# Four VectorE sums of a Strassen-Winograd product, handed out one at a time between out matmuls

## The chip, the core and the metric

The kernel runs on one core of a Trainium2 chip. The metric is the device time of one execution in microseconds (us), lower is better. A core has TensorE (PE, matmuls into PSUM), VectorE (DVE), ScalarE (ACT, activations), GpSimd (POOL) and SyncE (SP); each works through a queue of its own in order, and they wait for one another by semaphores. PSUM has eight banks, each of which holds one matmul output of 128 x 512 float32.

## The reference

Sigmoid attention over 8 batches of 12 heads, 448 positions and 64 channels a head, followed by a feed-forward layer with SiLU on the 3584 x 768 result:

```python
scores = scale * np.matmul(q, k.transpose(0, 1, 3, 2)) - np.log(S)
attn = 1.0 / (1.0 + np.exp(-scores))
attn_out = np.matmul(attn, v)
...
x = np.ascontiguousarray(attn_out.transpose(0, 2, 1, 3)).reshape(B * S, H * D)
h = x @ w_in
g = h * (1.0 / (1.0 + np.exp(-h)))
return (g @ w_out).astype(np.float32)
```

w_in is 768 x 2048 and w_out 2048 x 768. All is computed in float16 with float32 sums; the result is float32.

## The kernel before

**Stages.** Heads are taken in groups g of four (three groups make a batch, 24 groups in all), and a group's scores in seven units (`NCH`), so that a batch pair has 42 units. The pairs are worked through in stages. A first stretch does the attention of the first pair, then h of its two batches runs as plain products with the attention of the second pair between. Then the loop at the end of the kernel runs three times, m = 0, 1, 2. Each pass has an *out stage*: the out products of pair m (`sets(m)`, g @ w_out), with the attention of pair m + 1 between them. Then comes an *h stage*: `h_pair(m + 1)`, x @ w_in with SiLU for that pair. A last `sets(3)` ends the kernel.

**Out stage.** In `out_set` a set of two row blocks is computed with seven products instead of eight (Strassen-Winograd): each is eight matmuls of 128x128 by 128x384 into one PSUM bank `po`. In this text they are P1 to P7. VectorE reads each out of its bank: P1 at L511 (`m1`), P2 at L515, P3 at L521, P4 at L525, P5 at L528, P6 at L531 and L532, P7 at L536. It also makes the four sums S1 to S4 of `gTr` (L509, L512, L516, L522), which are weights of later products; S4 of L522 is for P7. In the out stages with attention, `banks_for_attention(3)` gives three double banks to scores and P·V, and leaves two single banks for `po`, taken in turn. So a product's first matmul waits for the eviction of the product two before it.

**Attention between.** `burst(n)` issues the scores of two units (`scores`, eight matmuls for the two, then one sigmoid of ScalarE per unit) and, one burst after a group's last unit, the group's P·V (`values`, 28 matmuls), whose two results VectorE writes to `xT` (L267). Behind a burst the loop takes `int(behind_burst)` steps from the stream of out matmuls: `few` behind a burst with values (2 in m = 0 and 2, 4 in m = 1), `many` behind another (8.5 and 11.4 on average). `rows_if_any` is called twice in each round: right behind the burst, and in the middle of its out matmuls. It hands out the copies and transposes of later rows of k and q, where such wait in `later`.

**The sums of x.** h of a pair is a Strassen-Winograd product too, and needs four sums of `xT`: `tx[m, 1]`, `tx[m, 2]`, a sum in place of `x1[0]`, and `tx[m, 4]` (L352 to L355, here s1 to s4; s2 reads s1, s4 reads s2). `xT` has six channel groups of 128, of which each attention group g fills two. The first two thirds of the sums (`x_sums(m, 0, NQ - 1)`, 128x896 each) can be made when the last but one attention group of the pair is in; `after_values` issues all four there, behind that group's `values`. The last third (128x448 each) is made within the h stage by `last_values`, behind the last group's values; `gate` then lets GpSimd go on to the next rows and loads.

The order of instructions on each engine is the order in which the program issues them.

Of the kernel before, what the change touches and what calls it, by code (L numbers as in the profile page):

```python
# [17 lines left out]
def kernel(  # L18
# [9 lines left out]
    nc = tc.nc  # L28
# [8 lines left out]
    NQ = NPAIR // 2  # L37
# [26 lines left out]
    def banks_for_attention(doubles):  # L64
        psum.close()
        banks.clear()
        bufs_of.update(double=doubles, single=NBANK - 2 * doubles)
        for name, bufs in bufs_of.items():
            taken[name] = 0
            new_pool(name, bufs)  # L70
# [7 lines left out]
    def banks_for_h():  # L78
        doubles = [[2 * i, 2 * i + 1] for i in longest_idle("double")]
        ring[:] = sum(doubles[:-2], [])  # L80
        ring.extend(2 * bufs_of["double"] + i for i in longest_idle("single"))
        ring.extend(sum(doubles[-2:], []))
        psum.close()
        banks.clear()
        new_pool("any", 1)
        for i in range(NBANK):
            banks[i] = banks["any"].tile([P, 512], F32, tag=f"any{i}", name=f"any{i}")
# [32 lines left out]
    def load(names, g, c0=0, c1=NCH):  # L120
        for name in names:
            if (name, g) not in flat:
                new_flat(name, g)
            nc.gpsimd.dma_start(  # L124
                flat[name, g][:, :, c0:c1].rearrange("p i c d -> p i (c d)"),
                rows_in(name, g)[:, :, c0 * D : c1 * D],
            )
# [22 lines left out]
    def load_w_in(step):  # L150
        cols = slice(step * DFF // 4, (step + 1) * DFF // 4)
        rows = moe_w_in[:, cols].rearrange("(iq j h d) f -> h j d iq f", j=2, h=2, d=D)
        for half in range(2):
            for j in range(2):
                nc.gpsimd.dma_start(
                    w_in_sb[j * D : (j + 1) * D, half * NQ : (half + 1) * NQ, cols], rows[half, j]
                )

    def load_w_out(nh, part):
        cols = slice(nh * NO2, (nh + 1) * NO2)  # L160
        fcs = slice(part * NFC // 2, (part + 1) * NFC // 2)
        nc.gpsimd.dma_start(
            w_out_sb[:, fcs, cols],
            moe_w_out[part * DFF // 2 : (part + 1) * DFF // 2, cols].rearrange(
                "(fc p) e -> p fc e", p=P
            ),
        )
# [39 lines left out]
    def dma_transpose(g, name, copy):  # L207
        if ("k", g) not in qkT:
            new_qkT(g)
        rows = p2.tile([P, NCH, 2, D], F16, tag=f"{name}r", name=f"{name}r")  # L210
        copy(rows, flat[name, g].rearrange("p j c d -> p c j d"))
        nc.sync.dma_start_transpose(
            out=qkT[name, g], in_=rows.rearrange("p c j d -> p (c j d)")
        )
# [62 lines left out]
    def room_x():  # L277
        return p3.tile([P, NQ, S], F16, tag="tx", name="tx")
# [64 lines left out]
    tx = {}  # L343

    def x_sums(m, lo, hi):
        if lo == 0:
            for i in (1, 2, 4):
                tx[m, i] = room_x()
        of = slice(lo, hi)
        x0, x1 = ([xT[2 * m + j][:, c * NQ : (c + 1) * NQ] for c in range(2)] for j in range(2))  # L350
        sub = nc.vector.tensor_sub
        sub(tx[m, 1][:, of], x1[0][:, of], x0[0][:, of])  # L352
        sub(tx[m, 2][:, of], x1[1][:, of], tx[m, 1][:, of])  # L353
        sub(x1[0][:, of], x1[1][:, of], x1[0][:, of])  # L354
        sub(tx[m, 4][:, of], x0[1][:, of], tx[m, 2][:, of])  # L355

    NG = NFC // 2

    def h_pair(m, last_values):

        x0, x1 = xT[2 * m], xT[2 * m + 1]
# [68 lines left out]

        last = NG - 1
        order = [(m1, 0), (m1, 1), (last_values,), (m1, 2)]
        for i in range(3):
            order += [(m2, i), (silu11, i)]
# [132 lines left out]
    def sets(m):  # L567
        for g in range(0, NCH - 1, 2):
            step = out_set(
                block(m, g), row_blocks(m, g), block(m, g + 1), row_blocks(m, g + 1)  # L570
            )
            for i, ns in enumerate(step):
                if m == 0 and g == 0 and i in (10, 14):
                    next(sums)
                if m == 0 and g == 0 and i in (20, 28, 36, 44):
                    next(in_sums)
                yield ns
        if m % 2 == 1:
            g = NCH - 1
            yield from out_set(  # L580
                kept, row_blocks(m - 1, g), block(m, g), row_blocks(m, g), m == B // 2 - 1
            )

    later = []

    def rows_if_any(before, copy):
        if later and later[0][0] < before:
            g, name = later.pop(0)
            dma_transpose(g, name, copy)
            if name == "q":  # L590
                behind_rows(g, before)
# [3 lines left out]
    def behind_rows(g, before):  # L595
        if g + 3 >= NQB:
            return
        if g + 3 < before:
            load("kq", g + 3)
            return  # L600
        held.append(g + 3)
        if g + 1 == before:
            nc.gpsimd.tensor_copy(gate, qkT["q", g][:1, 0, :1])
            for to in held:
                load("kq", to)
            held.clear()
# [33 lines left out]
    def after_values(g):  # L640
        if g == 0:
            load("v", 3)
            load_w_in(2)
            load_w_in(3)
        elif g == 1:
            load("v", 4)
            load_w_out(0, 0)
            load_w_out(0, 1)
        elif g == 2:
            load("v", 5)  # L650
            load_w_out(1, 0)
            load_w_out(1, 1)
            load("kq", 6)
            load("kq", 7)
        elif g + 3 < NQB:
            load("v", g + 3)
        if g >= 2 * NQ and g % (2 * NQ) == 2 * NQ - 2:
            x_sums(g // (2 * NQ), 0, NQ - 1)

    def values_if_any():  # L660
        if waiting:
            g = waiting.pop(0)
            values(g)
            after_values(g)
            return True
        return False
# [15 lines left out]
    def rounds(g, end):  # L682
        values(g, end)
        if end == NCH:
            after_values(g)
# [47 lines left out]
    def burst(n):  # L733

        new = units[n : n + 2]
        for u in new:
            scores(*u)
        with_values = values_if_any()
        for g, ch in new:
            if ch == NCH - 1:  # L740
                waiting.append(g)
                if 9 <= g + 3 < NQB:
                    later.extend(((g + 3, "k"), (g + 3, "q")))
        return with_values
# [13 lines left out]
    for m in range(B // 2 - 1):  # L758
        banks_for_attention(3)
        nc.scalar.activation(warm, bias_s, AF.Sigmoid)  # L760
        stream = sets(m)
        for _ in range(FIRST_DENSE):
            next(stream)

        dense = (3 + m % 2) * 7 * NHC - FIRST_DENSE - ENDING
        with_values = 2 * NQ - 1
        few = 2 + 2 * (m % 2)
        many = (dense - with_values * few) / (NT_B - with_values)
        own = 2 * NQ * (m + 2)
        behind_burst = 0.0  # L770
        for n in range(2 * NT_B * (m + 1), 2 * NT_B * (m + 2), 2):
            behind_burst += few if burst(n) else many
            rows_if_any(own, nc.vector.tensor_copy)
            half = int(behind_burst) // 2
            for i in range(int(behind_burst)):
                next(stream)
                if i == half:
                    rows_if_any(own, nc.vector.tensor_copy)
            behind_burst -= int(behind_burst)
        nc.scalar.activation(warm, bias_s, AF.Silu)  # L780
        for _ in stream:
            pass
        (g,) = waiting
        waiting.clear()
        banks_for_h()
        values(g, NCH - 1)

        def last_values():
            values(g)
            after_values(g)  # L790
            x_sums(m + 1, NQ - 1, NQ)
            nc.gpsimd.tensor_copy(gate, tx[m + 1, 4][:1, NQ - 1, :1])

        for i, _ in enumerate(h_pair(m + 1, last_values)):
            if i % 8 == 7:
                rows_if_any(NQB, nc.gpsimd.tensor_copy)
# [33 lines left out]
```

## Time and profile before

| | us |
|---|---|
| median of 3 runs | 373.86 |
| lowest and highest run | 373.62, 374.12 |
| the profiled execution | 374.06 |
| its span, first to last instruction | 372.1 |

In a page of the profile the engines' busy time comes first, then groups of equal instructions, each with its line, engine, output and input tiles, count, busy time, mean length in ns, and the idle time of the engine just before them with what ended it. The timeline lists instructions of one engine in order of time, equal neighbours merged. The clock granted to TensorE was 0.999 over the span.

The groups that matter here beside those shown further on:

| line, engine, form | count | mean, ns |
|---|---|---|
| L352 to L355, DVE, 128x896 float16 | 3 each | 616 to 625 |
| L352 to L355, DVE, 128x448 float16 | 3 each | 382 to 393 |
| L521, L525, L528, DVE, 128x384 float32 | 14 each | 552 to 557 |
| L522, DVE, 128x1024 float16 | 14 | 681 |
| L267, DVE, 128x448 from PSUM | 48 | 619 |
| L501, PE, 128x384 | 784 | 326 to 327, one every 163 ns in a run of them |

### The profile page before, as it was taken

Reading aid. Unit: us, or ns where it says so; the run is one execution under the profiler, and the core shown is the slowest. Engines: PE = TensorE matmul, PEld = TensorE weight load, DVE = VectorE, ACT = ScalarE, POOL = GpSimd, SP = SyncE. Lnnn points to the kernel's source line nnn. Section 1 sums busy time; section 2 is a strip of 40 time slices with the busy share of each in tenths; the row PEclk is TensorE's granted clock in tenths of the full one; section 3 lists DMA queues with packets and bytes.
Section 4 is the critical chain, followed back from the end, with each engine's and each line's share of the span. In section 5 each row is a group of like instructions: output and inputs, shape, how many; then the busy total and the mean of one; then the engine's idle time right before and its main releaser. Section 6 shows DMA issues by size and latency. Waiting matters only on the chain. (4 is left out here: it accounts for less than half of the span.)

```text
span 372.1 us, 7598 instructions
## 1 busy us (share of the span) xinstructions
PE 360.6 (97%) x3009; PEld 179.8 (48%) x3009; DVE 252.0 (68%) x458; ACT 250.9 (67%) x339; POOL 77.5 (21%) x116
## 2 busy tenths in 40 slices
PE   7999999999999999999999899999999999999995
PEld 3554445544444455544444345554444445555553
DVE  2565469867566587867665658796665667797763
ACT  5998885479989655687778656679899846650000
POOL 8566521040060172000033036100100000000000
PEclk9999999999999999999999999999999999999999
DMA  8999999998789599008579459921983030003333
GB/s 135 192 204 204 204 203 204 181 127 154 132 106 218 115 122 177 2 0 158 93 136 181 113 110 143 120 37 26 175 108 88 0 87 0 3 0 85 86 85 85
DMA packets 65698, 42.78 MB, mean 115 GB/s; under 512 B 36096, under 2 KB 62208, under 8 KB 65664
## 3 DMA queue, kind: packets, MB, share of 16 engines
q0 software_dynamic: 27072, 22.58, 42.2%
q1 hardware_dynamic: 38240, 19.44, 27.2%
q8 instruction: 23, 0.38, 0.4%
q10 hardware_dynamic: 352, 0.30, 0.2%
q14 instruction: 11, 0.09, 0.1%
HBM read 45.61 MB, written 11.01 MB: 152 GB/s over the span
## 5 line engine op out<-in xcount | busy, mean ns | idle before, releaser
L232 ACT ACTIVATE attnT<-psc,bias_s 128x896 f16<-128x896 f32 x168 | 159.1, 1007 | 23.4 <-PE psc L225 22.9
L501 PEld LDWEIGHTS <-S 128*128 128x128 f16 x448 | 40.8, 98 | 39.6 <-issue 13.5
L225 PE MATMUL psc<-qT,kT 64*64 64x448 f16 x672 | 50.9, 362 | 1.5 <-ACT qT L186 0.6
L267 DVE TENSOR_SCALAR xT<-pav 128x448 f16<-128x448 f32 x48 | 27.7, 619 | 32.0 <-PE pav L256 32.0
L124 POOL DMA_DIRECT2D vf<-in_v_dram x24 | 17.3, 729 | 135.2 <-PE pav L256 130.6
L501 PEld LDWEIGHTS <-gTr 128*128 128x128 f16 x336 | 30.8, 98 | 30.2 <-issue 12.2
L501 PE MATMUL po<-T,S 128*128 128x384 f16 x224 | 42.5, 327 | 0.0
L501 PE MATMUL po<-w_out_sb,gTr 128*128 128x384 f16 x224 | 42.2, 327 | 0.0
L501 PE MATMUL po<-w_out_sb,S 128*128 128x384 f16 x224 | 40.4, 326 | 1.8 <-DVE osb L525 1.8
L375 PEld LDWEIGHTS <-w_in_sb 128*128 128x128 f16 x288 | 27.7, 98 | 26.9 <-issue 1.7
L256 PE MATMUL pav<-attnT,vf 64*64 64x448 f16 x672 | 38.9, 351 | 0.4 <-DVE gTr L303 0.4
L288 PE MATMUL ph<-xT,w_in_sb 128*128 128x448 f16 x192 | 38.7, 353 | 0.1
L375 PE MATMUL pa<-xT,w_in_sb 128*128 128x448 f16 x144 | 33.2, 353 | 0.0
L375 PEld LDWEIGHTS <-SI 128*128 128x128 f16 x216 | 21.1, 98 | 20.0 <-issue 0.5
L225 PEld LDWEIGHTS <-kT 64*64 64x64 f16 x672 | 15.4, 104 | 29.3 <-issue 25.7
L256 PEld LDWEIGHTS <-vf 64*64 64x64 f16 x672 | 21.4, 106 | 14.0 <-issue 5.4
L391 ACT ACTIVATE part<-pa 128x448 f32<-128x448 f32 x24 | 13.0, 543 | 21.5 <-PE pa L375 20.6
L288 PEld LDWEIGHTS <-w_in_sb 128*128 128x128 f16 x192 | 17.8, 98 | 19.1 <-issue 3.7
L501 PE MATMUL po<-T,gTr 128*128 128x384 f16 x112 | 22.2, 327 | 1.5 <-DVE osb L521 1.5
L369 ACT ACTIVATE gTr<-pc 128x448 f16<-128x448 f32 x24 | 13.0, 543 | 12.9 <-DVE pc L385 12.5
L385 DVE TENSOR_TENSOR part<-pb,part 128x448 f32<-128x448 f32 x24 | 14.9, 621 | 8.3 <-ACT part L391 5.0
L186 ACT ACTIVATE m<-po 128x384 f32<-128x384 f32 x1 | 0.5, 490 | 27.7 <-PE po L501 27.7
(76 smaller groups left out, 468.0 us busy)
## 6 DMA issues: line engine op xcount, KB each, us to landing
out_dram<-osb SPq DMA_DIRECT2D x54, 192.0 KB, 2.9
vf<-in_v_dram POOLq DMA_DIRECT2D x24, 224.0 KB, 7.0
kf<-in_k_dram POOLq DMA_DIRECT2D x23, 224.0 KB, 8.0
qf<-in_q_dram POOLq DMA_DIRECT2D x23, 224.0 KB, 8.5
w_in_sb<-in_moe_w_in_dram POOLq DMA_DIRECT2D x16, 192.0 KB, 7.9
w_out_sb<-in_moe_w_out_dram POOLq DMA_DIRECT2D x4, 768.0 KB, 14.9
kT<-kr SPq DMA_TRANSPOSE x18, 4.5
qT<-qr SPq DMA_TRANSPOSE x18, 4.8
```

The lines of the kernel that those rows point to most:

```text
L124: nc.gpsimd.dma_start(flat[name, g][:, :, c0:c1].rearrange("p i c d -> p i (c d)"), rows_in(name, g)[:, :, c0 * D : c1 * D],)
L186: nc.scalar.activation(o, i, AF.Copy)
L225: nc.tensor.matmul(psc[own, j, :S], qkT["k", g][rows, ch, own], qkT["q", g][rows, :, own], start=True, stop=True,)
L232: nc.scalar.activation(attnT[g, ch], psc[:, :, :S], AF.Sigmoid, bias=bias_s, scale=QKSCALE)
L256: nc.tensor.matmul(pav[half][j * D : (j + 1) * D, :S], flat["v", g][own, j, ch, :], at[own, j, :], start=(ch == 0), stop=(ch == NCH - 1),)
L267: nc.vector.tensor_scalar_mul(xT[b][:, half * NQ + iq, :], pav[half][:, :S], SX)
L288: nc.tensor.matmul(ph[:, :S], w_in_sb[:, cc, fc * P : (fc + 1) * P], xT[b][:, cc, :], start=(at == 0), stop=(at == NCC - 1),)
L369: nc.scalar.activation(gTr[:, r * NG + i, col + c * S : col + (c + 1) * S], h, AF.Silu, bias=0.0, scale=ISX)
L375: nc.tensor.matmul(to, w[:, n, i * P : (i + 1) * P], x[:, n], start=(start and n == 0), skip_group_check=not start, stop=(n == NQ - 1),)
L385: nc.vector.tensor_add(o, po, x)
L391: nc.scalar.activation(got[i, 1], bank[i, "a"], AF.Copy)
L501: nc.tensor.matmul(po[:, :NO2], a[:, fc, :], w[:, fc, :], start=(fc == 0), stop=(fc == NHC - 1))
```

## The change

`x_sums` becomes a generator that yields behind each of its sums. At the place where the four sums were issued, the generator is now put into a list, `sums_of_x`, and every call of `rows_if_any` takes one step of it, ahead of what it did before. The first step is thus taken right behind the burst whose values completed the group, the second in the middle of the out matmuls behind that burst, the third behind the next burst, the fourth in the middle of that burst's out matmuls. The last third's sums in `last_values` are run through at once, as before. What is computed stays the same.

```diff
         of = slice(lo, hi)
         x0, x1 = ([xT[2 * m + j][:, c * NQ : (c + 1) * NQ] for c in range(2)] for j in range(2))
-        sub = nc.vector.tensor_sub
-        sub(tx[m, 1][:, of], x1[0][:, of], x0[0][:, of])
-        sub(tx[m, 2][:, of], x1[1][:, of], tx[m, 1][:, of])
-        sub(x1[0][:, of], x1[1][:, of], x1[0][:, of])
-        sub(tx[m, 4][:, of], x0[1][:, of], tx[m, 2][:, of])
+        for o, x, y in (
+            (tx[m, 1], x1[0], x0[0]),
+            (tx[m, 2], x1[1], tx[m, 1]),
+            (x1[0], x1[1], x1[0]),
+            (tx[m, 4], x0[1], tx[m, 2]),
+        ):
+            nc.vector.tensor_sub(o[:, of], x[:, of], y[:, of])
+            yield
...
-    later = []
+    later, sums_of_x = [], []
 
     def rows_if_any(before, copy):
+        if sums_of_x and next(sums_of_x[0], "end") == "end":
+            sums_of_x.pop()
         if later and later[0][0] < before:
...
         if g >= 2 * NQ and g % (2 * NQ) == 2 * NQ - 2:
-            x_sums(g // (2 * NQ), 0, NQ - 1)
+            sums_of_x.append(x_sums(g // (2 * NQ), 0, NQ - 1))
...
             behind_burst -= int(behind_burst)
+        assert not sums_of_x
         nc.scalar.activation(warm, bias_s, AF.Silu)
...
             values(g)
             after_values(g)
-            x_sums(m + 1, NQ - 1, NQ)
+            for _ in x_sums(m + 1, NQ - 1, NQ):
+                pass
             nc.gpsimd.tensor_copy(gate, tx[m + 1, 4][:1, NQ - 1, :1])
```

## The prediction

> **What bounds the kernel now.** I read the page's busy table first, then its groups of instructions, then the waits, then the timeline of VectorE and TensorE around the four sums.
>
> ```profile
> PE 360.6 (97%) x3009; PEld 179.8 (48%) x3009; DVE 252.0 (68%) x458; ACT 250.9 (67%) x339; POOL 77.5 (21%) x116
> ...
> L501 PE MATMUL po<-w_out_sb,S 128*128 128x384 f16 x224 | 40.4, 326 | 1.8 <-DVE osb L525 1.8
> ...
> L501 PE MATMUL po<-T,gTr 128*128 128x384 f16 x112 | 22.2, 327 | 1.5 <-DVE osb L521 1.5
> ```
>
> TensorE is busy for 97% of the span, so whatever shortens the kernel has to take away either matmuls or a gap of TensorE. The last column of the two groups is the idle time just before them: 1.8 + 1.5 us in which out products stood still until VectorE had emptied a bank (L525, L521). In the timeline of TensorE these are three gaps, 0.88 us at 120.5, 1.49 us at 209.35 and 0.87 us at 293.6, one in each out stage that has attention beside it (m = 0, 1, 2), and they are its only gaps after 48 us: together 3.24 us. I call the seven products of an out set P1 to P7, and the four sums s1 to s4 (L352 to L355). Two banks serve the products, so P5 waits until P3 is read (L521), P6 until P4 is read (L525), and P7 until P5 is read (L528).
>
> Stage m = 0, VectorE and then TensorE (columns: start, length, instruction, idle time before it and what ended it):
>
> ```profile
> 117.45 1.16 DVE L267 TENSOR_SCALAR xT<-pav 128x448 f16<-128x448 f32 x2 [1.50 <-PE pav L256]
> 118.53 0.62 DVE L352 TENSOR_TENSOR tx<-xT 128x896 f16<-128x896 f16 x1
> 119.18 0.63 DVE L353 TENSOR_TENSOR tx<-xT,tx 128x896 f16<-128x896 f16 x1
> 119.72 0.62 DVE L354 TENSOR_TENSOR xT<-xT 128x896 f16<-128x896 f16 x1
> 120.25 0.62 DVE L355 TENSOR_TENSOR tx<-xT,tx 128x896 f16<-128x896 f16 x1
> 120.79 0.55 DVE L525 TENSOR_TENSOR osb<-po,osb 128x384 f32<-128x384 f32 x1
> 121.44 0.55 DVE L528 TENSOR_TENSOR osb<-osb,po 128x384 f32<-128x384 f32 x1
> ```
>
> ```profile
> 120.18 0.34 PE L501 MATMUL po<-T,gTr 128*128 128x384 f16 x1
> 121.39 2.76 PE L501 MATMUL po<-w_out_sb,S 128*128 128x384 f16 x16 [0.88 <-DVE osb L525]
> ...
> 294.48 2.76 PE L501 MATMUL po<-w_out_sb,S 128*128 128x384 f16 x16 [0.87 <-DVE osb L525]
> ```
>
> VectorE runs without a hole from 117.45 to L525's end at 121.34. P4 was finished at about 118.6 (its last matmul starts at 118.27), so L525 stands behind the sums and waits for nothing but its turn; P6 starts 0.05 us after its end. Stage m = 2 has the same order: there L525 starts at 293.87 and P6 at 294.48.
>
> Stage m = 1:
>
> ```profile
> 207.97 0.62 DVE L352 TENSOR_TENSOR tx<-xT 128x896 f16<-128x896 f16 x1
> 208.62 0.62 DVE L353 TENSOR_TENSOR tx<-xT,tx 128x896 f16<-128x896 f16 x1
> 209.16 0.62 DVE L354 TENSOR_TENSOR xT<-xT 128x896 f16<-128x896 f16 x1
> 209.70 0.62 DVE L355 TENSOR_TENSOR tx<-xT,tx 128x896 f16<-128x896 f16 x1
> 210.23 0.55 DVE L521 TENSOR_TENSOR osb<-po,m 128x384 f32<-128x384 f32 x1
> 210.70 0.68 DVE L522 TENSOR_TENSOR S<-gTr,S 128x1024 f16<-128x1024 f16 x1
> 211.30 0.55 DVE L525 TENSOR_TENSOR osb<-po,osb 128x384 f32<-128x384 f32 x1
> ```
>
> ```profile
> 208.04 1.31 PE L501 MATMUL po<-T,S 128*128 128x384 f16 x7
> 210.84 0.81 PE L501 MATMUL po<-T,gTr 128*128 128x384 f16 x4 [1.49 <-DVE osb L521]
> ...
> 212.75 1.46 PE L501 MATMUL po<-w_out_sb,S 128*128 128x384 f16 x8
> ```
>
> Here the sums fall one product earlier, so P3's L521 is the one that stands behind them, and P5 waits 1.49 us. P6 follows at 212.75 without a gap, since L525 was done at 211.85.
>
> **The change part by part.** *Nothing is added or removed.* The built programs have equal numbers of instructions, and TensorE, ScalarE, GpSimd and SyncE keep theirs in the same order with the same waits; no DMA moves past another. Only VectorE's queue differs, in three places. In m = 0 and m = 2 the order s1, s2, s3, s4, L525, L528 becomes s1, s2, s3, L525, s4, L528. In m = 1 the order s1, s2, s3, s4, L521, L522, L525 becomes s1, L521, L522, s2, s3, s4, L525. The sums of the last third stay together.
>
> *m = 0 and m = 2: L525 passes one sum.* It starts where s4 now starts, at 120.25 and not 120.79: 0.54 us earlier. P6 starts at 121.39 - 0.54 = 120.85, and the gap falls from 0.88 to 0.34 us. In m = 2, s4's start is 293.34 against L525's 293.87: 0.53 us, gap 0.34. L525 also waits for the store that last read its buffer; that store belongs to the set before, whose last eviction started at 107.0 (280.1 in m = 2), and stores land a median of 2.9 us after issue, at most 7.3. That is some 5 us of cover.
> Next in the queue, s4 now stands ahead of L528. L525 to the next start takes 0.47 us when nothing is waited for (as L521 to L522 in m = 1), so s4 starts at 120.72, L528 some 0.54 later at 121.26 and ends at 121.81. P7 needs that when P6 is done, 1.30 us after 120.85 (8 matmuls at 0.163), at 122.15. Cover: 0.34 us, so this costs nothing. s4's result is read by the h stage ten microseconds on.
>
> *m = 1: L521 and L522 pass three sums.* The start-to-start times come from the rows above and from the neighbours in the same queue: sum to eviction 0.53 (209.70 to 210.23), L521 to L522 0.47, L522 to a next one 0.60 (210.70 to 211.30), sum to sum 0.54. So L521 starts at 207.97 + 0.53 = 208.50 and ends at 209.05. P3 is done by about 207.5, so it is not held. P5 is ready at 210.84 - 1.49 = 209.35, and finds its bank free: the 1.49 us are gone. But L525 now has everything ahead of it: L522 at 208.97, s2 at 209.57, s3 at 210.11, s4 at 210.65, L525 at 211.18 to 211.73, only 0.12 us before its old time. P6 is ready 1.91 us after P5's start (212.75 - 210.84, with the scores between), at 211.26, and must wait until 211.73 + 0.06 = 211.79. **A new gap of 0.53 us takes the place of the old one**, and the gain here is 1.49 - 0.53 = 0.96 us. After it L528 and P7 have the same distances as today.
>
> *Bounds of the new neighbourhoods.* No row shows a sum directly before L522 or L522 directly before a sum. If each of the six steps from s1 to L525 took the shortest start-to-start of these rows, 0.47, L525 would end 0.39 us earlier (6 x 0.47 = 2.82 against 3.21) and the gap be 0.14: gain 1.35. If each took the whole length of its instruction (0.62, 0.55, 0.68, 0.62, 0.62, 0.62 = 3.71), L525 would end at 212.23 and the gap be 1.03: gain 0.46. I take the middle values, since each is the row of the very same pair of kinds.
>
> By the rows, an instruction of VectorE starts 0.08 us before the end that is shown of the one ahead. The Trainium skill, "VectorE: DVE Perf Modes", section "The DRAIN you can't avoid", says that the next operation does not start until the pipe of the one before has emptied; it adds that one that is not held starts earlier. Read strictly, it speaks against the tight packing above; what that would do is the second rival below.
>
> *Is the gain kept to the end?* Behind each gap TensorE runs on without a hole, up to the next of the three. What does not move with it has room: in m = 0 ScalarE is at the sigmoids until 122.08 (118.26 + 3.82), then loads its table and runs a small call until 123.59, and the first work it takes from the h stage starts at 126.19, 2.59 us after it came free. That is much more than 0.54. The loads behind the h stage are released by the last third's s4 through `gate`, so they come earlier too.
>
> *Sum.* 0.54 + 0.96 + 0.53 = 2.03 us. The profiled execution took 374.06 us with a span of 372.1; the span should become 370.1 and that execution 372.0. Against the median of the runs, 373.86: **371.8 us**, 0.54% less. Runs lay within 0.25 us of the median on either side, and about 0.2% (0.75 us) is what can be told from no change.
>
> **The rivals.**
> *All three gaps close* (chance 0.05): if the distance between VectorE's starts were shorter than all rows say, up to 3.24 us would go: 370.6. Against it: in m = 0 the remaining 0.34 us are three sums and two evictions that still stand ahead of L525.
> *Whole lengths* (0.09): VectorE starts each instruction only at the end of the one before wherever the kinds change. Then m = 1 gains 0.46 and the sum is 0.54 + 0.46 + 0.53 = 1.53 us: 372.3. For it: L352 to L353 is 0.65, the whole length. Against: the pairs sum to eviction (0.53 at a length of 0.62), eviction to S sum (0.47 at 0.55) and S sum to eviction (0.60 at 0.68) are all in the rows, and all overlap. The DRAIN section of the Trainium skill's page "VectorE: DVE Perf Modes", read strictly, is this case.
> *The wait moves and the gain goes back* (0.08): TensorE, earlier by 2 us, meets something that keeps its own time, a transposed k or q for instance, and the end stays: 373.9. For it: GpSimd waits 5.7 us in all for transposes to land in the h stages. Against: TensorE waits for no DMA at all after 19 us, and those transfers hang on the same chain. Half given back would be 372.8.
> *Slower: s4 holds L528 and P7* (0.06). Place: m = 0 and m = 2, where s4 is now between L525 and L528, with a wait of its own. If it were held for W beyond its row, P7 would start W - 0.34 late, and the stage loses once W is above 0.34 + 0.54 = 0.88 us. For the longest wait of VectorE in this stretch, 2.25 us (for P·V of the last third at 127.0), it would be 2 x (2.25 - 0.88) - 0.96 = 1.78 us more: 375.6. Against it: s4 waits only for s2, which is an eviction and a sum back in the same queue.
> That the sums don't spread at all is excluded, since the order of the built program shows the three moves.
>
> **How the numbers follow.** Forecast 0.72, and 0.05, 0.09, 0.08, 0.06 for the rivals in their order. The predicted time is the forecast's, 371.8. Its bounds: 2.42 us gained (0.54 + 1.35 + 0.53) gives 371.4, 1.53 us gives 372.3; with 0.25 us of the runs and a little for the half that may be given back, 371.0 to 372.7, which holds the forecast and the second rival, 0.81. Faster by over 0.2%: 0.72 + 0.05 + 0.09 = 0.86. Within 0.2%: 0.08. Slower: 0.06.
>
> **What would show it.** Right: three waits of TensorE for evictions of 0.34, 0.53 and 0.34 us, the middle one now before P6 and for the eviction of P4; none before P5; L525 in m = 0 and 2 at the old start of s4; every later instruction 0.5, 1.5 and 2.0 us earlier behind the three places. Wrong: a gap before P7 in m = 0 or 2 (slower rival), a gap near 1.0 us before P6 in m = 1 (whole lengths), or a new gap of TensorE later on with a DMA or ScalarE as its releaser. If the gaps shrink as said and the time does not, the explanation of the bound is wrong.

## The result, and the profile after

| | before | after |
|---|---|---|
| median, us | 373.96 (6 runs) | 371.90 (6 runs) |
| lowest to highest, us | 373.62 to 374.12 | 371.60 to 372.24 |
| ratio, 95% interval | | 0.9946 (0.9934 to 0.9959) |
| span of the profiled execution, us | 372.1 | 369.9 |
| gaps of TensorE after 48 us, us | 0.88 + 1.49 + 0.87 = 3.24 | 0.34 + 0.52 + 0.34 = 1.20 |

The change saves 2.06 us, 0.54%. In the changed kernel all four sums have line L357, and the evictions stand three lines lower: L521, L525 and L528 of before are L524, L528 and L531. The page's busy table and the two groups of out products that stood still before:

```profile
PE 360.6 (97%) x3009; PEld 179.9 (49%) x3009; DVE 251.8 (68%) x458; ACT 251.0 (68%) x339; POOL 77.5 (21%) x116
...
L504 PE MATMUL po<-w_out_sb,S 128*128 128x384 f16 x224 | 40.4, 326 | 1.2 <-DVE osb L528 1.2
...
L504 PE MATMUL po<-T,gTr 128*128 128x384 f16 x112 | 22.2, 327 | 0.0
```

TensorE is busy for the same 360.6 us as before, and VectorE within 0.2 us: no work went away. What went away stands in the last column. P5 (`T,gTr`) no longer waits, and P6 (`w_out_sb,S`) waits 1.2 us over three stages.

The timeline of VectorE in m = 0 (start, length, instruction):

```profile
119.60 0.62 DVE L357 TENSOR_TENSOR xT<-xT 128x896 f16<-128x896 f16 x1
120.13 0.55 DVE L528 TENSOR_TENSOR osb<-po,osb 128x384 f32<-128x384 f32 x1
120.60 0.62 DVE L357 TENSOR_TENSOR tx<-xT,tx 128x896 f16<-128x896 f16 x1
121.13 0.55 DVE L531 TENSOR_TENSOR osb<-osb,po 128x384 f32<-128x384 f32 x1
```

and in m = 1:

```profile
207.31 0.62 DVE L357 TENSOR_TENSOR tx<-xT 128x896 f16<-128x896 f16 x1
207.84 0.55 DVE L524 TENSOR_TENSOR osb<-po,m 128x384 f32<-128x384 f32 x1
208.31 0.68 DVE L525 TENSOR_TENSOR S<-gTr,S 128x1024 f16<-128x1024 f16 x1
208.91 0.62 DVE L357 TENSOR_TENSOR tx<-xT,tx 128x896 f16<-128x896 f16 x1
209.45 0.62 DVE L357 TENSOR_TENSOR xT<-xT 128x896 f16<-128x896 f16 x1
209.98 0.62 DVE L357 TENSOR_TENSOR tx<-xT,tx 128x896 f16<-128x896 f16 x1
210.52 0.55 DVE L528 TENSOR_TENSOR osb<-po,osb 128x384 f32<-128x384 f32 x1
```

The timeline of TensorE at the three places, with the idle time and what ended it in brackets:

```profile
120.74 2.76 PE L504 MATMUL po<-w_out_sb,S 128*128 128x384 f16 x16 [0.34 <-DVE osb L528]
...
208.53 0.81 PE L504 MATMUL po<-T,gTr 128*128 128x384 f16 x4
...
211.12 2.76 PE L504 MATMUL po<-w_out_sb,S 128*128 128x384 f16 x16 [0.52 <-DVE osb L528]
...
292.32 2.76 PE L504 MATMUL po<-w_out_sb,S 128*128 128x384 f16 x16 [0.34 <-DVE osb L528]
```

In m = 0 the eviction of P4 (L528) stands one sum earlier in VectorE's queue and P6 follows it. In m = 1 the eviction of P3 (L524) now stands ahead of the last three sums, P5 starts at 208.53 without a bracket, and the wait that is left has moved one product on, to P6. From P6 of m = 2 to the end of the span it is 77.6 us in both kernels (372.1 - 294.48, 369.9 - 292.32): nothing was given back.

### The profile page after: what moved, and what is told of

It reads as the page before. It is cut to its first block, busy times and chain, and to the rows that moved or that the text cites. A ratio compares the mean times of both kernels' runs of the same rounds, so it can differ in the third digit from the quotient of the medians.

```text
span 369.9 us, 7597 instructions
## 1 busy us (share of the span) xinstructions
PE 360.6 (97%) x3009; PEld 179.9 (49%) x3009; DVE 251.8 (68%) x458; ACT 251.0 (68%) x339; POOL 77.5 (21%) x116
## 4 chain that ended last, share of the span: by engine, by line
PE 85%; DMA 7%; DVE 4%; POOL 1%; issue 1%; ACT 0%; DVEq 0%
PE po L504 35%; PE psc L225 9%; PE pav L256 8%; PE pa L378 8%; PE pd L378 7%; PE pc L378 7%; DMA w_out_sb<-in_moe_w_out_dram 5%; PE ph L288 5%; PE pb L378 4%; DMA vf<-in_v_dram 2%; PE pw L183 2%; DVE xT L267 1%; DVE tx L357 1%; POOL w_out_sb L162 1%; PE ptrq L196 1%
```

## The experiments

The theory was the prediction's: TensorE stands still because evictions queue behind the sums on VectorE, and each stage's gap counts by itself. The first four runs share 14 runs of the kernel before (median 374.08), the last four share 15 others (373.72).

**The parts alone.** Two kernels use the generator in some stages and run it through at once in the others:

```diff
-            sums_of_x.append(x_sums(g // (2 * NQ), 0, NQ - 1))
+            step = x_sums(g // (2 * NQ), 0, NQ - 1)
+            if g // (2 * NQ) == 2:
+                sums_of_x.append(step)
+            else:
+                for _ in step:
+                    pass
```

(`== 2` is the out stage m = 1; the second kernel has `!= 2`.)

> Only the out stage m = 1 hands the sums out one at a time; m = 0 and m = 2 issue all four at once as before. Theory (TensorE stands still for evictions queued behind the sums, each stage by itself): gaps 0.88, 0.53 before P6, 0.87; gain 0.96 us, 372.9 to 373.0 against 373.9. Rival (the gain comes from one thing shared by the stages, so that a part alone brings nothing or nearly all): 373.9 or 371.9.

Measured: 372.85 us, ratio 0.9973 (0.9962 to 0.9983), gaps 0.87, 0.52 and 0.88.

> Only the out stages m = 0 and m = 2 hand the sums out one at a time; m = 1 issues all four at once as before. Theory: gaps 0.34, 1.49 before P5, 0.34; gain 0.54 + 0.53 = 1.07 us, 372.8 to 372.9 against 373.9. With the run of m = 1 alone it should add up to 2.0 us. Rival: no sum of the parts.

Measured: 372.79 us, ratio 0.9968 (0.9957 to 0.9979), gaps 0.34, 1.49 (before P5) and 0.34. The two ratios multiply to 0.9941, against 0.9946 for the whole change. Against the 374.08 that they share, the parts gain 1.23 and 1.29 us where 0.96 and 1.07 were expected; both forecasts lie within the intervals, and the gaps are as forecast. Each stage's gain is its own, and the parts add up.

**More of the suspected cost.** The kernel before, with s1 made twice:

```diff
         sub(tx[m, 1][:, of], x1[0][:, of], x0[0][:, of])
+        if lo == 0:
+            sub(tx[m, 1][:, of], x1[0][:, of], x0[0][:, of])
```

> The kernel before, with the first sum s1 made twice (the same result) ahead of the other three in each of the three out stages. Theory: each eviction behind the sums comes one sum later, gaps 0.88 + 0.54, 1.49 + 0.54, 0.87 + 0.54; 1.6 us slower, 375.5. Rival (VectorE's time is hidden here and the shorter gaps of the changed kernel have another cause): within 0.2 us of 373.9.

Measured: 376.64 us, ratio 1.0073 (1.0057 to 1.0090). Its gaps in TensorE's timeline:

```profile
122.18 2.76 PE L503 MATMUL po<-w_out_sb,S 128*128 128x384 f16 x16 [1.53 <-DVE osb L527]
...
212.28 0.81 PE L503 MATMUL po<-T,gTr 128*128 128x384 f16 x4 [2.15 <-DVE osb L523]
...
296.58 2.76 PE L503 MATMUL po<-w_out_sb,S 128*128 128x384 f16 x16 [1.53 <-DVE osb L527]
```

Each gap grew by 0.65 us and not by 0.54, because the second s1 writes what the first wrote and starts only 0.65 after it (119.30 after 118.65). That makes 5.21 us of gaps, 1.97 more than before: 376.05. Three executions at a granted clock of 1.0 took 375.72, 375.73 and 376.13 and fit; the three others had a mean clock of 0.993 and took 377.15 to 377.23. So time added on VectorE at this place is paid in full; the 1.2 us more at a lower clock were followed up below.

**The evictions first.** The changed kernel, with s3 and s4 handed out two calls later:

```diff
-    later, sums_of_x = [], []
+    later, sums_of_x, sums_now = [], [], [None]
 
     def rows_if_any(before, copy):
-        if sums_of_x and next(sums_of_x[0], "end") == "end":
-            sums_of_x.pop()
+        if sums_of_x and sums_of_x.pop(0):
+            next(sums_now[0], None)
...
-            sums_of_x.append(x_sums(g // (2 * NQ), 0, NQ - 1))
+            sums_now[0] = x_sums(g // (2 * NQ), 0, NQ - 1)
+            sums_of_x.extend((1, 1, 0, 0, 1, 1))
```

> The changed kernel with the third and fourth step two calls later: the orders become s1, s2, L525, s3, L528, s4 in m = 0 and 2 and s1, L521, L522, s2, L525, s3, L528, s4 in m = 1 (line numbers of the kernel before). Theory: L525 ends at 120.27 in m = 0 where P6 is ready at 120.5, and at 210.66 in m = 1 where P6 is ready at 211.26; all three gaps close, 3.24 us less than before, 370.6 to 370.7, 1.2 below the changed kernel. Rival (s3 or s4 now holds L528, and the wait moves from P6 to P7): P7 gaps of 0.1 to 0.5 us, 371.5 or more. Second rival (the sums come too late for the h stage): a gap of TensorE at the first product that reads them.

Measured: 370.12 us, ratio 0.9899 (0.9887 to 0.9912). In VectorE's timeline of m = 1 two sums are behind L528, the eviction of P4, and TensorE's has no gap after 48 us. VectorE there, then P5 and P6:

```profile
208.61 0.55 DVE L528 TENSOR_TENSOR osb<-po,osb 128x384 f32<-128x384 f32 x1
209.08 0.61 DVE L357 TENSOR_TENSOR xT<-xT 128x896 f16<-128x896 f16 x1
...
210.27 0.62 DVE L357 TENSOR_TENSOR tx<-xT,tx 128x896 f16<-128x896 f16 x1
```

```profile
207.69 0.81 PE L504 MATMUL po<-T,gTr 128*128 128x384 f16 x4
...
209.60 2.76 PE L504 MATMUL po<-w_out_sb,S 128*128 128x384 f16 x16
```

P6 starts 1.91 us behind P5 and has no bracket. No wait moved to P7 or into the h stage: both rivals fall. But it saves 3.96 us, more than the 3.24 that the gaps showed. From P6 of m = 0 to P6 of m = 1, without the gap, it is 89.87 us before (212.75 - 121.39 - 1.49) and 89.70 here (209.60 - 119.90). The next stretch, from there to P6 of m = 2, shrinks by 0.17 too, from 80.86 (294.48 - 212.75 - 0.87) to 80.69 (290.29 - 209.60). So each of these two gaps, closed altogether, gives 0.17 us more than it showed, about one slot of an out matmul (0.163). The run with the sums on GpSimd, below, shows the same 89.70 and 80.69.

**What a shown gap leaves out.** The same kernel with the steps `(1, 1, 0, 1, 0, 1)`, which in m = 1 puts s3 ahead of L528 again:

> As the run with two sums behind the eviction, but in m = 1 s3 goes ahead of L525 (s1, L521, L522, s2, s3, L525, L528, s4, by the line numbers of the kernel before); m = 0 and 2 keep their order. L525 then ends about 0.54 later, and P6 is ready 1.91 us behind P5's start. By shown gaps alone (prediction: ready at 211.26, bank free at 211.25) nothing changes: 370.1, P5's start to P6's start 1.91. Rival from the last runs (TensorE could start 0.163 us before the shown end of the last matmul, so a shown gap understates the wait by that much): P6 starts 2.05 us behind P5 with a shown gap of about 0, and the time is 0.1 us longer.

The eviction of P4 on VectorE in m = 1, then P5 and P6 on TensorE:

```profile
209.70 0.55 DVE L528 TENSOR_TENSOR osb<-po,osb 128x384 f32<-128x384 f32 x1
```

```profile
208.25 0.81 PE L504 MATMUL po<-T,gTr 128*128 128x384 f16 x4
...
209.50 0.82 PE L504 MATMUL po<-T,gTr 128*128 128x384 f16 x4
210.31 2.76 PE L504 MATMUL po<-w_out_sb,S 128*128 128x384 f16 x16
```

P6 starts 2.06 us behind P5 instead of 1.91, and 0.06 us behind the end of the eviction at 210.25: it waited for its bank. Yet no idle time is shown: the four matmuls from 209.50 are drawn up to 210.32. They go out one every 0.163 us but are drawn 0.326 long, so the next could have started at 210.15. The rival is right, to 0.01 us. The time, 370.22 us (ratio 0.9906, 0.9893 to 0.9920), can't be told from 370.12; the timeline decides.

**The cover at P7.** The changed kernel with s4 made twice:

```diff
             nc.vector.tensor_sub(o[:, of], x[:, of], y[:, of])
+            if lo == 0 and o is tx[m, 4]:
+                nc.vector.tensor_sub(o[:, of], x[:, of], y[:, of])
             yield
```

> The changed kernel with s4 made twice (the same result) in each of the three stages, the second time right behind the first. It spends the cover that the prediction gave for P7: in m = 0 and 2 the eviction of P5 comes 0.65 later (a sum that writes what the one before wrote took 0.65 from start to start in the run with one sum more). Theory: 0.31 of that is covered (eviction's end at 121.68 and 0.05, P7 ready 8 x 0.163 behind P6's start at 120.74, 122.04), so P7 is 0.34 late in m = 0 and 2 (a shown gap of 0.18, since the shown end of a matmul lies 0.163 behind the slot of the next), and in m = 1 P6's gap grows from 0.52 to 1.17: 1.3 us slower than the changed kernel, 373.2. Rival (s4's place is harmless, its time always hidden): 371.9; rival (no cover at P7): 373.9.

Measured: 373.44 us, ratio 0.9988 (0.9980 to 0.9997). In TensorE's timeline of m = 0, P6 and then P7 (L530 and L533 are the evictions of P4 and P5 here):

```profile
120.96 1.46 PE L506 MATMUL po<-w_out_sb,S 128*128 128x384 f16 x8 [0.34 <-DVE osb L530]
122.62 1.46 PE L506 MATMUL po<-w_out_sb,S 128*128 128x384 f16 x8 [0.20 <-DVE osb L533]
```

P7 now starts 1.66 us behind P6 and not 1.30: 0.36 late for 0.65 us of added work, so 0.29 was covered. m = 2 shows the same 0.34 and 0.20, and m = 1 a gap of 1.18 before P6. The interval puts this kernel 0.1 to 0.75 us below the kernel before, so one repeated sum takes back most of what the change gained. The theory's 373.2 lay 0.7 below the 373.9 that it was set against, inside that; a time that is always hidden would be 2.0 below, and no cover at all 0: both are outside.

**The sums on another engine.** The kernel before, with the first two thirds' sums on GpSimd:

```diff
-        sub = nc.vector.tensor_sub
+        sub = nc.gpsimd.tensor_sub if lo == 0 else nc.vector.tensor_sub
```

> The kernel before with the four sums of the first two thirds made by GpSimd instead of VectorE, all four at once. Theory (what costs time is that evictions queue behind the sums, not that the sums are made): all three gaps of TensorE close, 370.1 to 370.4 as in the run with two sums behind the eviction, as long as GpSimd is done when the h stage reads the sums (it has 8.9 us free before its next load; a 128x896 copy takes it 0.92 us). Rival (GpSimd needs over 2 us for a sum of two inputs, and holds up VectorE's evictions or the h stage): gaps before P5, P6 or before the first product with tx, 372 or more.

Measured: 369.89 us, ratio 0.9895 (0.9881 to 0.9909), no gap of TensorE after 48 us. A sum takes GpSimd 1.87 to 2.23 us, but its four are done by 125.9 in m = 0, and the h stage waits for none of them. VectorE did not go untouched. GpSimd and VectorE in m = 1:

```profile
206.75 1.90 POOL L352 TENSOR_TENSOR tx<-xT 128x896 f16<-128x896 f16 x1
208.73 2.23 POOL L353 TENSOR_TENSOR tx<-xT,tx 128x896 f16<-128x896 f16 x1
```

```profile
206.82 0.55 DVE L521 TENSOR_TENSOR osb<-po,m 128x384 f32<-128x384 f32 x1
207.28 1.93 DVE L522 TENSOR_TENSOR S<-gTr,S 128x1024 f16<-128x1024 f16 x1
```

L522 took 1.93 us and not 0.68: it ended 0.56 us after GpSimd's first sum did. GpSimd's second sum, at work while L522 ended, is the one that took 2.23 us and not 1.88. L521, beside the first sum, took its usual 0.55. The eviction behind L522 was done by 209.69, and P6 was ready at 209.94, so it cost nothing here.

**Longer gaps and the clock.** The kernel before with s1 made four times:

```diff
         sub(tx[m, 1][:, of], x1[0][:, of], x0[0][:, of])
+        for _ in range(3 if lo == 0 else 0):
+            sub(tx[m, 1][:, of], x1[0][:, of], x0[0][:, of])
         sub(tx[m, 2][:, of], x1[1][:, of], tx[m, 1][:, of])
```

> The kernel before with s1 made four times in each of the three stages. By gaps alone: three starts of 0.65 more in each stage, gaps 2.84, 3.45 and 2.84, 380.0. In the run with one sum more, three of six executions had a mean granted clock of 0.993 and took 1.2 us longer than its gaps of 1.53, 2.15 and 1.53 account for. If a gap of TensorE of 2 to 3 us makes the clock drop for a while, this run shows a clock below 1 behind the gaps in its profile, and takes up to 3 x 1.2 us more, 381 to 384; if that was something else, 380.0 at a clock of 1.0.

Measured: 385.19 us (381.43 to 385.85), ratio 1.0306 (1.0287 to 1.0325). Gaps 2.85, 3.46 and 2.85, as expected. The profiled execution is the fastest, 381.43 us at a mean clock of 0.994. Its busy time in stretches (us of the stretch; PE, PEld, DVE, ACT, POOL busy; granted clock; DMA's share and GB/s) around the gap of m = 1:

```profile
206.00:214.80 8.80, 5.39 (x62) 2.53 (x61) 6.88 (x13) 4.64 (x5) 0.72 (x1) 0.98 0.59 138
214.80:217.00 2.20, 2.15 (x12) 0.59 (x11) 1.07 (x2) 0.08 (x1) 0.00 (x0) 0.50 0.00 0
217.00:219.00 2.00, 2.00 (x14) 1.07 (x11) 0.55 (x1) 1.98 (x3) 0.00 (x0) 0.78 0.00 0
219.00:221.00 2.00, 2.00 (x16) 1.08 (x18) 1.08 (x3) 1.33 (x2) 0.00 (x0) 1.00 0.00 0
```

Behind the 3.46 us gap TensorE worked at half clock for some 3 us. Its two gaps of 2.85 us were followed by full clock in this execution; the other four executions had a mean clock of 0.981 to 0.985 and took 383.93 to 385.85. One drop makes 0.994 here, so by the clock these fit two or three drops each, but none of them was profiled. The median lies above the 381 to 384 us expected, which allowed 1.2 us for each of three drops; the one drop in the profile went with 1.4 us over the 380.0 of gaps alone, and what the rest is stays open. The Trainium skill, "TensorE: Matmul & The Clock Gate", section "HAM oscillation — how this bites in real kernels", names gaps of more than about 3.4 us as those to avoid; the 3.46 us gap agrees. The clock of 0.993 with gaps of at most 2.15 us, in half of the executions of the run with one sum more, would not, if those gaps are what caused it; that is not shown.

## Why the prediction was right

| step | predicted, us | measured, us |
|---|---|---|
| m = 0 and 2: gap before P6 | 0.34, 0.34 | 0.34, 0.34 |
| m = 1: gap before P5 | none | none |
| m = 1: new gap before P6 | 0.53 | 0.52 |
| cover at P7 | 0.34 | 0.29 (s4 twice) |
| time, against the median of before | -2.03 | -2.06 |

*The bound.* That TensorE's three gaps are evictions behind the sums was shown both ways: they grew when a sum was added, closed when the sums were put behind the evictions, and closed when the sums left VectorE's queue while all of its evictions stayed.

*The moves.* The starts in the new order are those added up beforehand: sum to eviction 0.53, eviction to S sum 0.47, S sum to sum 0.60, sum to sum 0.53 to 0.54 in m = 1. The rival of whole lengths falls with them: L524 starts 0.53 behind a sum that lasts 0.62. By the Trainium skill's "The DRAIN you can't avoid" ("VectorE: DVE Perf Modes"), read strictly, it could not; the section's own addition, that an operation which is not held starts earlier, fits, and the trace decides. Whole lengths do appear where an instruction needs, or overwrites, what the one just before wrote (0.65 in the runs with s1 or s4 repeated).

*The slower rival.* s4 started 0.47 us behind the eviction ahead of it and was not held. Its place is not free, though: 0.29 us more on VectorE there was all that could be hidden.

*Kept to the end.* The tail behind the last gap is unchanged, and the two runs without gaps, 4.0 and 3.8 us shorter than the kernel before, show nothing else that comes to bind. Of the 2.2 us that the profiled span lost, 0.13 stand ahead of the first gap (P5 of m = 0 starts at 118.32 and not 118.45) and are not the change's; the rest is what the gaps give.

*What was not quite right, and cancelled.* In m = 1 the prediction took P5 as ready at 209.35, the old start less the shown gap. It was ready one slot earlier, at 209.19 (210.84 - 1.49 - 0.16). So closing that gap gained 1.65 us, and P6 then lost 0.68 (211.12 against 208.53 + 1.91), of which 0.52 shows. The difference, 0.97, is what was forecast as 1.49 - 0.53 = 0.96, because one gap took the place of another. For the same reason the rival in which all gaps close was priced some 0.5 us too high, at 370.6; the two kernels that closed them took 370.12 and 369.89.

## What to carry to other kernels

A short burst of work that nobody waits for costs TensorE time if a PSUM eviction that a coming matmul needs is queued behind it on the same engine, though that engine was busy for only 68% of the span here. What it costs is the part that reaches beyond the moment when that matmul is ready: four sums of some 2.2 us showed gaps of 0.87 to 1.49 us, and whatever was added to them then cost its full length. Ask of such work how many evictions it should let pass, not only whether it is spread. Here one at a time gained 0.54%, and holding the last two sums back for two calls more gained 1.0%, since one at a time had still left three or four sums ahead of P4's eviction. A wait that is shortened in part can come back one product on, so follow the banks for two more products before adding up the gain.

## What the hardware showed that was not expected

- A gap of TensorE in the timeline is short by one matmul slot, 0.16 us for 128x384 here, because the timeline draws a matmul longer than the time to the next. A wait of up to that length is not shown at all (2.06 us for 1.91 between P5 and P6, with no idle time).
- A gap of TensorE can cost more than its length: half clock for some 3 us behind one of 3.46 us, while the gaps of 2.85 us in the same profile were followed by full clock. Three executions with gaps of 1.53, 2.15 and 1.53 us took 1.2 us longer at a mean clock of 0.993; where in those the clock fell, and that a gap caused it, was not seen.
- A VectorE sum of two float16 SBUF inputs was held up beside a GpSimd sum (1.93 us for 0.68, seen once), while evictions from PSUM beside it were not (0.55 to 0.56).
